# A gated mix of an S4 convolution and a two-token expert layer on one core: padded one-hot rows, spectra spread in place, a reloaded input, chunked expert weights, a split last block and new planner ranks

## The chip, the cores and the metric

The kernel runs on one core of a Trainium2 chip. The metric is the device time of one execution in microseconds (us), as the median of several runs. The profile is one further execution, taken by the hardware profiler; its times count from the first instruction.

## The reference, cut to what matters

The input `u` has 2048 time steps and 512 channels. Three results are mixed:

```
g = sigmoid((x * gate_w).sum(-1))                  # one gate per time step
a = conv(u, K) + u * Dskip                         # K[d,l] = Re sum_n C dB exp(dt A l)
r = x @ w_r;  idx = two largest of r               # the router picks 2 time steps
y = (silu(x[idx] @ w_gate) * (x[idx] @ w_up)) @ w_down * sigmoid(r[idx])
b = x + y scattered to the rows idx
out = g * a + (1 - g) * b
```

The convolution has 2048 taps per channel, each a sum over 128 complex states; the reference does it with an FFT of length 4096. The expert layer has a hidden width of 1792 and sees two rows only.

## The kernel before, in words

**Stages.** The channels are worked on in two halves of 256 (`h` = 0, 1), the time steps in two blocks of 1024 (`blk` = 0, 1).

1. ScalarE (ACT) and VectorE (DVE) build powers of the states: exponentials and sines (L638, L646, L721, L738) on ACT, their arguments (L643, L732) and the complex products (L617, L652, L668, L671) on DVE. ACT changes its function table between exponentials and sines.
2. TensorE (PE) transforms the input with a DFT matrix (L789, L792, tiles `x`), ACT evicts it (L796), and DVE forms sums and differences of the rows ("spread", L802), out of place from the tiles `eo` into the tiles `x`.
3. For each half PE multiplies the powers into taps (L838, L839; evicted L851), selects and regroups them (L863), and transforms them into the spectrum of the taps, `Kh` (L896; evicted L901), with the matrices `km`, loaded once for both halves (L811).
4. The router: PE transposes the input (L925), ACT evicts it (L928), PE forms the logits (L936). A chain of small steps on DVE, ACT and PE finds the two largest (L980 to L995), writes them as two one-hot columns into `oht` (L990, L996), transposes these to two rows `ohr` (L1013, L1016), gathers the two input rows by matmul against the input `u` (L1023), and runs the expert layer: L1050 for gate and up, L1056 to L1061 for the silu, L1066 for down, then three small steps that leave the result in row 0 and 1 of the tile `zb` (L1071 to L1073).
5. For each half and block, DVE multiplies the spectra ("Y", 16 or 8 operations over 128x2048 in bf16) and folds them; PE transforms back ("inv"): for each of 8 row groups one matmul adds the skip path (L1136), one adds the expert rows by the one-hot rows and `zb` (L1137), and eight are the transform (L1140). ACT scales (L1148) and SyncE (SP) stores.

**What sets the order.** Nothing is ordered by hand. Every operation is a node of a graph. A planner (L219) simulates the engines with a cost for each node, gives each engine the ready node of the highest rank (`RANKS`, L37) whose tiles fit into the SBUF, and so fixes the order of each engine's instructions and the waits between them (L324). On the chip each engine then runs its list strictly in order. The planner's SBUF budget is 4096 bytes a partition below the whole. `after=` adds a dependence: the loads of the expert weights, of the inverse DFT matrix and of the second copy of the input (L1078) come after the last tap matmul of the second half (`TAP1`); both sigmoids of the router wait for the last sine of the second half (`SINS`, L962, L1001). Every transform back waits for `zb`, since L1137 is in its accumulation group.

Of the kernel before, what the change touches and what calls it, by code (L numbers as in the profile page):

```python
# [24 lines left out]
MAGIC = 12582912.0  # L25
SB_BYTES = 212832


def bf16_bits(x):
# [55 lines left out]
class Op:  # L85
    __slots__ = ("name", "opts", "preds", "succs", "tiles", "prio", "npred", "ready", "eng", "start",
                 "fin", "idx", "mem", "dma", "bytes", "final", "num", "i", "pref", "clock")
# [35 lines left out]
def pack(tiles, size):  # L123

    near = {}
    for t in tiles:
        near[t.name] = [d for d in tiles if d is not t and d.t0 < t.t1 and t.t0 < d.t1]
    best = None
    for key in (lambda t: (-t.size * (t.t1 - t.t0), t.t0), lambda t: (-t.size, t.t0), lambda t: (-(t.t1 - t.t0), -t.size), lambda t: (t.t0, -t.size)):
        order = sorted(tiles, key=key)  # L130
        for _ in range(150):
            pos, top, worst = {}, 0, None
            for t in order:
                a = 0
                for lo, hi in sorted((pos[d.name], pos[d.name] + d.size) for d in near[t.name] if d.name in pos):
                    if a + t.size <= lo:
                        break
                    a = max(a, hi)
                pos[t.name] = a
                if a + t.size > top:  # L140
                    top, worst = a + t.size, t
            if best is None or top < best[0]:
                best = (top, pos)
            if top <= size:
                break
            k = order.index(worst)
            order.pop(k)
            order.insert(k // 2, worst)
        if best[0] <= size:
            break  # L150
    for t in tiles:
        t.addr = best[1][t.name]
    return best[0]


class Graph:
# [20 lines left out]
    def op(self, name, opts, reads=(), writes=(), pref=None, bias=0.0, after=(), hold=()):  # L177
        o = Op()
# [3 lines left out]
        o.i = len(self.ops)  # L182
        for a in after:
            o.preds[a.i] = a
# [34 lines left out]
    def schedule(self):  # L219
        ops = self.ops  # L220
# [21 lines left out]
        t = 0.0  # L242
        events = set()
        while left:
# [3 lines left out]
            while progress:  # L248
                progress = False
                for e in ENGS:  # L250
# [57 lines left out]
            if not nxt:  # L308
                if left:
                    w = sorted((o.name, [tl.name for tl in o.tiles if tl.t0 is None]) for e in ENGS for o in avail[e])  # L310
                    live = [(tl.name, tl.size) for tl in self.tiles if tl.t0 is not None and tl.t1 is None and tl.space == "sb"]
                    raise RuntimeError("no way on at %.1f: %s; live %s" % (t, w[:20], live))
                break
# [5 lines left out]
        if self.used > SB_BYTES:  # L319
            raise RuntimeError("needs %d bytes" % self.used)  # L320
        for tl in sb:
            tl.before = [o for d in sb if d.t1 <= tl.t0 and d.addr < tl.addr + tl.size and tl.addr < d.addr + d.size for o in d.ops]

# [155 lines left out]
def bass_gated_mix__ssm_conv_s4__moe_arch_mod__prompt_kernel(nc, A_u, A_A_re, A_A_im, A_B_re, A_B_im, A_C_re, A_C_im, A_log_dt, A_Dskip,  # L479
# [27 lines left out]
    with ExitStack() as es:  # L507
# [205 lines left out]
        for h in range(2):  # L713
# [27 lines left out]
            SINS = sins  # L741
            g.op("k0 im", {POOL: (lambda hh, ti=ti: hh.memset(ti(BF, 0, 128, 0, (128, NG), (1, 4)), 0.0), 0.5)}, [], [bk[0]], bias=100, after=sins[8:9])
# [27 lines left out]
        tEO = [[T("eo%d_%d" % (b, ri), 8192) for ri in range(2)] for b in range(2)]  # L770
        bEO = [[[Buf(tEO[b][ri]) for _ in range(4)] for ri in range(2)] for b in range(2)]
        tX = [[T("x%d_%d" % (b, ri), 8192) for ri in range(2)] for b in range(2)]
        bX = [[[Buf(tX[b][ri]) for _ in range(2)] for ri in range(2)] for b in range(2)]

        def eov(b, ri, row, *dims):
            return tEO[b][ri](BF, 0, 128, row * D, *dims)
        for b in range(2):
            for ri in range(2):
                for pr in range(4):
                    ps = PS("ps_x%d_%d_%d" % (b, ri, pr), 2)  # L780
                    bp = [Buf(ps) for _ in range(2)]
                    for i in range(2):
# [3 lines left out]
                        def mm(h, ps=ps, i=i, eo=eo, ri=ri, ft=ft, b=b, row=row):  # L786
# [8 lines left out]
                        XD.append(g.op("X%d row%d.%d" % (b, ri, row), {PE: (mm, 0.216 * (5 if b else 4))}, rd, [bp[i]], hold=[tEO[b][ri]]))  # L795
                    g.op("ev X%d.%d.%d" % (b, ri, pr), {ACT: (lambda h, ps=ps, b=b, pr=pr, ri=ri: h.activation(out=eov(b, ri, 2 * pr, (1, 1024)), in_=ps(F32, 0, 128, 0, (1, 1024)), func=ACTF.Copy), ca(1024, True)),  # L796
                                                        DVE: (lambda h, ps=ps, b=b, pr=pr, ri=ri: h.tensor_copy(eov(b, ri, 2 * pr, (1, 1024)), ps(F32, 0, 128, 0, (1, 1024))), cd(1024, x=2))},
                         bp, [bEO[b][ri][pr]], pref=ACT)
        for b in range(2):
            for ri in range(2):  # L800
                for sd in range(2):
# [408 lines left out]
```

## Time and profile before

| what | us |
|---|---|
| median of 3 runs (213.28 to 215.01) | 213.92 |
| the profiled execution's own time | 211.22 |
| its span, first to last instruction | 209.4 |
| DVE busy | 155.0 |
| PE busy | 145.9 |
| ACT busy | 136.0 |
| mean granted clock of PE | 0.868 of 2.4 GHz |

The profile page gives busy time by engine and in 40 slices; the queries of the trace give the chain of waits that ended last, the busy time of each engine in chosen stretches, and the instructions of an engine in order of time. A busy PE is not PE at its peak, since matmuls overlap; the distance from one start to the next is what a matmul costs.

### The profile page before, as it was taken

Reading aid. Unit: us, or ns where it says so; the run is one execution under the profiler, and the core shown is the slowest. Engines: PE = TensorE matmul, PEld = TensorE weight load, DVE = VectorE, ACT = ScalarE, POOL = GpSimd, SP = SyncE. Lnnn points to the kernel's source line nnn. Section 1 sums busy time; section 2 is a strip of 40 time slices with the busy share of each in tenths; the row PEclk is TensorE's granted clock in tenths of the full one; section 3 lists DMA queues with packets and bytes.
Section 4 is the critical chain, followed back from the end, with each engine's and each line's share of the span. In section 5 each row is a group of like instructions: output and inputs, shape, how many; then the busy total and the mean of one; then the engine's idle time right before and its main releaser. Section 6 shows DMA issues by size and latency. Waiting matters only on the chain.

```text
span 209.4 us, 3594 instructions
## 1 busy us (share of the span) xinstructions
PE 145.9 (70%) x1479; PEld 99.1 (47%) x1482; DVE 155.0 (74%) x249; ACT 136.0 (65%) x260; POOL 2.1 (1%) x10
## 2 busy tenths in 40 slices
PE   0508959972973894994011698997055999999993
PEld 0402424420453893872010697887012566666661
DVE  0497999949899999989798859999999993000000
ACT  2299999999699599799999595365003133333331
POOL 0000000000000000000000000000000000000000
PEclk9999999996797698899555599999558599999999
DMA  4994000000039300000000199992800011111111
GB/s 109 346 426 130 2 2 3 0 0 0 0 113 412 129 3 3 0 0 0 0 6 0 25 379 325 406 368 73 289 0 0 0 53 50 50 50 53 50 50 50
DMA packets 13923, 20.71 MB, mean 99 GB/s; under 512 B 4690, under 2 KB 10964, under 8 KB 12884
## 3 DMA queue, kind: packets, MB, share of 16 engines
q1 hardware_dynamic: 12564, 20.01, 26.8%
q10 hardware_dynamic: 1344, 0.49, 1.0%
q8 instruction: 11, 0.18, 0.3%
q14 instruction: 4, 0.03, 0.1%
HBM read 18.40 MB, written 2.10 MB: 98 GB/s over the span
## 4 chain that ended last, share of the span: by engine, by line
PE 42%; ACT 38%; DVE 13%; DMA 3%; issue 2%; ACTq 1%
PE RP L1140 16%; DVE RB L617 9%; ACT RB L721 8%; PE RP L896 7%; ACT RB L738 6%; ACT RB L796 5%; ACT RB L901 4%; PE RP L1137 3%; ACT RB L928 3%; DMA RB<-in_A_B_im_dram 3%; PE RP L838 3%; PE RP L839 2%; PE RP L1066 2%; ACT RB L638 2%; PE RP L1136 2%
## 5 line engine op out<-in xcount | busy, mean ns | idle before, releaser
L617 DVE TENSOR_TENSOR RB<-RB 128x2048 bf16<-128x2048 bf16 (+3 forms) x76 | 85.7, 1182 | 3.4 <-PE RP L839 1.8
L789 PE MATMUL RP<-RB 128*128 128x512 bf16 x125 | 34.4, 416 | 13.5 <-ACT RB L796 7.3
L1140 PE MATMUL RP<-RB 128*128 128x256 bf16 x256 | 35.8, 286 | 0.0
L1148 ACT ACTIVATE RB<-RP,RB 128x256 bf16<-128x256 f32 x32 | 13.4, 471 | 32.2 <-PE RP L1140 32.2
L789 PEld LDWEIGHTS RP<-RB 128*128 128x128 bf16 x128 | 12.9, 105 | 32.4 <-ACT RB L796 9.0
L896 PE MATMUL RP<-RB 128*128 128x256 bf16 x208 | 24.9, 283 | 4.4 <-ACT RB L874 3.6
L1140 PEld LDWEIGHTS RP<-RB 128*128 128x128 bf16 x256 | 23.4, 102 | 7.2 <-issue 0.7
L668 DVE TENSOR_TENSOR RB<-RB 128x1024 bf16<-128x1024 bf16 x40 | 25.2, 682 | 0.1
L896 PEld LDWEIGHTS RP<-RB 128*128 128x128 bf16 x208 | 20.7, 101 | 8.7 <-ACT RB L874 4.2
L721 ACT ACTIVATE RB<-RB 128x256 bf16<-128x256 f32 x62 | 20.3, 413 | 0.0
L901 ACT ACTIVATE RB<-RP 128x1024 bf16<-128x1024 f32 x16 | 15.8, 1030 | 6.5 <-PE RP L896 6.5
L738 ACT ACTIVATE RB<-RB 128x512 bf16<-128x512 int16 x32 | 17.6, 616 | 0.3 <-DVE RB L732 0.3
L796 ACT ACTIVATE RB<-RP 128x1024 bf16<-128x1024 f32 x16 | 15.5, 1012 | 1.6 <-PE RP L792 1.6
L838 PE MATMUL RP<-RB 128*128 128x84 bf16 x128 | 13.3, 224 | 4.0 <-DVE RB L617 2.6
L732 DVE TENSOR_SCALAR RB<-RB 128x256 int32<-128x256 f32 x49 | 11.7, 286 | 5.1 <-ACT RB L738 5.0
L838 PEld LDWEIGHTS RP<-RB 128*128 128x128 bf16 x128 | 12.6, 114 | 4.7 <-DVE RB L617 2.9
L851 ACT ACTIVATE RB<-RP 128x1008 bf16<-128x1008 f32 (+1 forms) x12 | 10.5, 910 | 4.4 <-PE RP L839 4.4
L839 PE MATMUL RP<-RB 128*128 128x84 bf16 x128 | 13.3, 223 | 0.0
L671 DVE TENSOR_TENSOR RB<-RB 128x1024 bf16<-128x1024 bf16 x20 | 12.9, 682 | 0.0
L839 PEld LDWEIGHTS RP<-RB 128*128 128x128 bf16 x128 | 12.6, 113 | 0.1
L1066 PE MATMUL RP<-RB 128*2 128x512 bf16 x14 | 4.9, 524 | 8.7 <-DVE RB L1061 8.7
L1136 PE MATMUL RP<-RB 128*128 128x256 bf16 x32 | 9.1, 286 | 2.2 <-ACT RB L955 2.2
(79 smaller groups left out, 147.0 us busy)
## 6 DMA issues: line engine op xcount, KB each, us to landing
RB<-in_A_u_dram SPq DMA_DIRECT2D x4, 1024.0 KB, 7.6
RB<-c_kspec SPq DMA_DIRECT2D x6, 512.0 KB, 6.4
RB<-c_fwd SPq DMA_DIRECT2D x2, 1024.0 KB, 9.6
RB<-c_inv SPq DMA_DIRECT2D x2, 1024.0 KB, 6.7
out_dram<-RB SPq DMA_DIRECT2D x8, 256.0 KB, 2.3
RB<-in_B_w_gate_dram SPq DMA_DIRECT2D x1, 1792.0 KB, 11.8
RB<-in_B_w_up_dram SPq DMA_DIRECT2D x1, 1792.0 KB, 15.7
RB<-in_B_w_down_dram SPq DMA_DIRECT2D x1, 1792.0 KB, 7.9
```

Source lines behind the costliest of these rows:

```text
L617: return g.op(name, {DVE: (lambda h: h.tensor_tensor(out=o(), in0=a(), in1=b(), op=op), cost)}, rd, wr, bias=bias, **kw)
L668: g.op("%s.m%d" % (name, i), {DVE: (lambda h, i=i, pa=pa, pb=pb: h.tensor_tensor(out=tv(i, inp_a[1]), in0=inp_a[0](pa), in1=inp_b(pb), op= ...
L721: e2.append(g.op("exp t1_%d %d" % (h, m), {ACT: (lambda hh, m=m, s=s, h=h: hh.activation(out=tT1[h](BF, 0, 128, s * 4, (128, NG), (1, 4)), ...
L738: sins.append(g.op("sin%d %d.%d" % (h, q, cs), {ACT: (lambda hh, ta=ta, cs=cs, tt_=tt_, q=q: hh.activation(out=tt_(BF, 0, 128, 8 * q, (4, ...
L789: r = h.matmul(o, tF(BF, 0, 128, ((j * 2 + ri) * 4 + ft) * 128, (1, 128)), tU(BF, 0, 128, (b * 8 + j) * D, (1, D)), start=(j == eo), stop= ...
L796: g.op("ev X%d.%d.%d" % (b, ri, pr), {ACT: (lambda h, ps=ps, b=b, pr=pr, ri=ri: h.activation(out=eov(b, ri, 2 * pr, (1, 1024)), in_=ps(F32 ...
L838: hh.matmul(o, tT1[h](BF, 0, 128, gr * 128, (1, 128)), t2v(h, 0, 0, (HC, NSL), (1, 4)) if gr == 0 else tT2[h](BF, 0, 128, 4 * gr, (HC, NSL ...
L839: r = hh.matmul(o, tTI[h](BF, 0, 128, gr * 128, (1, 128)), tT2[h](BF, 0, 128, NSL * HC + 4 * gr, (HC, NSL), (1, 4)), start=False, stop=True)
L896: r = hh.matmul(o, tKM[m](BF, 0, 128, c, (1, 128)), tKC[h](BF, 0, 128, u * 256, (1, 256)), start=(n == 0), stop=(n == len(steps) - 1))
L901: g.op("ev Kh %d.%d.%d" % (h, blk, pr), {ACT: (lambda hh, h=h, base=base, ps=ps: hh.activation(out=tKHH(h, base), in_=ps(F32, 0, 128, 0, ( ...
L1140: r = hh.matmul(o, tG(BF, 0, 128, ((j * 2 + ri) * 4 + ft) * 128, (1, 128)), tS(BF, 0, 128, (j % 2) * 2048 + ri * 1024 + ft * HC, (1, HC)), ...
L1148: r = hh.activation(out=tO(BF, 0, 128, i * 256, (1, 256)), in_=ps(F32, 0, 128, i * 256, (1, 256)), func=ACTF.Copy, scale=g32(0, 128, blk * ...
```

## The change

What it does, by parts: the one-hot columns stand 128 apart and the rows of `ohr` and `zb` are filled with zeros to 128 rows; the spread is written into one tile of nine 4096-byte slots that holds both the evicted transforms and the spread ones; the gather reads the second copy of the input, which is loaded after the first one-hot is there; the matrices `km` are loaded once for each half; the gate and up weights come in two chunks of columns each and the down weights in two chunks in tiles of their own, all after the last one-hot eviction (`GATE`); the router's sigmoids wait for the sines of the first half only (`SIN0`), the silu still for all; the last block (h = 1, blk = 1) is multiplied, folded and transformed back in two parts by frequency; the diagonal is made by 16 small operations. The planner gets new ranks, a larger SBUF margin (14336 bytes, raised until the tiles fit), another packing search, a cost for table loads and one for a cold PE. All ranks change; the diff shows a few.

```diff
-    ("tr u", 496), ("ev xt", 496), ("logits", 496), ... ("tr oh", 600), ("ev oh", 500), ("gather", 470), ... ("ffn", 470), ("h", 600), ... ("down", 600)
+    ("tr u", 926.9), ("ev xt", 810.0), ("logits", 810.0), ... ("tr oh", 356.6), ("ev oh", 348.1), ("gather", 925.3), ... ("ffn", 768.4), ("h", 803.1), ... ("down", 778.1)
-    ("Y0.0", 420), ("Y0.1", 410), ("inv 0", 400), ("ld w", 390), ("Y1.0", 320), ("Y1.1", 310), ("inv 1", 300)
+    ("Y0.0", 229.1), ("Y0.1", 509.1), ("inv 0", 303.0), ("ld w", 850.0), ("Y1.0", 848.4), ("Y1.1", 224.9), ("inv 1", 938.4)
...
+        for cut in range(CUT, 40000, 2048):
+            self.cap = SB_BYTES - cut
...
+                    if e == PE:
+                        if t - free[PE] > 3.0:
+                            warm = t + 5.0
+                        if t < warm:
+                            c = min(2 * c, c + (warm - t) / 2)
+                    if o.table and o.table != table:
+                        table = o.table
+                        c += 1.28
...
-        tEO = [[T("eo%d_%d" % (b, ri), 8192) for ri in range(2)] for b in range(2)]
-        tX = [[T("x%d_%d" % (b, ri), 8192) for ri in range(2)] for b in range(2)]
+        tXE = T("xe", 9 * 4096)
...
+                    over = (bEO[(i - 1) // 2][(i - 1) % 2][0:2] if i else []) if sd == 0 else bEO[b][ri][2:4]
+                    tt("spread %d.%d.%d" % (b, ri, sd), lambda xp=xp, sd=sd: tXE(BF, 0, 128, xp[sd] * 2048, (1, 2048)), ... bEO[b][ri], [bX[b][ri][sd]] + over, cd(2048))
...
-        tKM = [T("km%d" % u, 4096 if u < 6 else 2048, keep=430) for u in range(7)]
+        tKM = [[T("km%d_%d" % (u, h), 4096 if u < 6 else 2048, keep=(630, 490)[h]) for u in range(7)] for h in range(2)]
+            ld_km(h, xdone if h == 0 else T1DONE)
...
-        g.op("exp s", ..., [bSB], [bEx], after=SINS)
+        g.op("exp s", ..., [bSB], [bEx], after=SIN0)
...
-        dv("diag", lambda h: h.tensor_tensor(out=tDG(BF, 0, 128, 0, (128, 16), (1, 128)), ...
+            for tb in range(16):
+                r = h.tensor_scalar(out=tDG(BF, 0, 128, tb * 128, (1, 128)), in0=ident(), scalar1=rat(0, 128, tb, (1, 1)), scalar2=None, op0=ALU.mult)
...
-        tOH = T("oht", 64); bOH = Buf(tOH)
+        tOH = T("oht", 4096); bOH = Buf(tOH)
+        g.op("zero oh", {POOL: (lambda h: h.memset(tOH(BF, 0, 128, 0, (1, 2048)), 0.0), 2.5)}, [], [bOH], after=[LG0])
...
-                    r = h.transpose(ps(BF, 0, 2, i * 128, (1, 128)), tOH(BF, 0, 128, (hf * 8 + i) * 2, (1, 2)), ident())
+                    r = h.transpose(ps(BF, 0, 128, i * 128, (1, 128)), tOH(BF, 0, 128, (hf * 8 + i) * 128, (1, 128)), ident())
...
+        GATE = g.ops[-1:]
+            g.dma("ld U2_%d" % b, ..., 1048e3, writes=[bU2[b]], after=OH1)
-        g.op("gather", {PE: (gat, 4.8)}, bU + [bOH, bRatb], [bGt], bias=60)
+        g.op("gather", {PE: (gat, 2.3)}, bU2 + [bOH, bRatb], [bGt], bias=60)
-        tWG = T("wg", 14336); tWU = T("wu", 14336); tWD = tWG
+                tw = T("w%s%d" % ("gu"[i], c), 7168); bw = Buf(tw)
+                g.dma("ld w%s%d" % ("gu"[i], c), ..., 918e3, writes=[bw], after=GATE, bias=-10 * (2 * c + i))
+        tWD = [T("wd%d" % c, 7168) for c in range(2)]; bWD = [Buf(t) for t in tWD]
+            g.dma("ld wd%d" % c, ..., 918e3, writes=[bWD[c]], after=GATE, bias=-50 - 10 * c)
+        g.op("zero zb", {POOL: (lambda h: h.memset(tZB(BF, 0, 128, 1024, (1, D)), 0.0), 0.6)}, [], [bZB[2]], after=[LG0])
...
+                nparts = 2 if (h, blk) == (1, 1) else 1
+                nr = 4 // nparts
+                for pt in range(nparts):
...
-                                hh.matmul(o, tOR(BF, 0, 2, tb * 128, (1, 128)), tZB(BF, 0, 2, 1024 + h * HC, (1, HC)), start=False, stop=False)
+                                    if pt == 0:
+                                        hh.matmul(o, tDG(...), tU2[blk](...), start=(jj == 0), stop=False)
+                                        hh.matmul(o, tOR(BF, 0, 128, tb * 128, (1, 128)), tZB(BF, 0, 128, 1024 + h * HC, (1, HC)), start=False, stop=False)
+                                    for ft in range(pt * nr, pt * nr + nr):
```

## Rows read from the trace of the kernel before

**Rows 1.** The page, busy time by engine, and PE's granted clock in 40 slices.
```profile
PE 145.9 (70%) x1479; PEld 99.1 (47%) x1482; DVE 155.0 (74%) x249; ACT 136.0 (65%) x260; POOL 2.1 (1%) x10
...
PEclk9999999996797698899555599999558599999999
```

**Rows 2.** The chain of waits that ended last: start us, length us, what.
```profile
153.98 4.90 PE RP L1066 x14
...
161.06 0.40 PE RP L1136
...
205.81 0.47 ACT RB L1148
206.29 0.36 ACTq L507
```

**Rows 3.** Busy time by stretch: from:to, length, engines (instructions), PE clock, DMA share, GB/s.
```profile
0.00:113.80 113.80, 68.28 (x614) 42.55 (x617) 97.54 (x183) 99.60 (x187) 2.08 (x10) 0.86 0.22 77
113.80:174.40 60.60, 46.22 (x625) 35.29 (x626) 57.45 (x67) 25.46 (x48) 0.00 (x0) 0.81 0.45 166
...
161.00:205.80 44.80, 44.72 (x320) 29.59 (x320) 13.40 (x12) 12.59 (x31) 0.00 (x0) 0.93 0.14 42
...
130.00:140.00 10.00, 9.26 (x88) 8.16 (x85) 10.00 (x10) 4.95 (x8) 0.00 (x0) 1.00 1.01 408
```

**Rows 4.** DVE in order of time: start us, length us, instruction, count, idle before.
```profile
7.82 0.69 DVE L600 SCALAR_TENSOR_TENSOR RB<-RP,RB 128x512 f32<-128x512 bf16 x1 [7.82 <-PE RP L584]
...
92.77 2.49 DVE L668 TENSOR_TENSOR RB<-RB 128x1024 bf16<-128x1024 bf16 x4
...
142.12 2.28 DVE L972 TENSOR_TENSOR RB<-RB 128x2048 bf16<-128x2048 bf16 x1
144.33 5.76 DVE L617 TENSOR_TENSOR RB<-RB 128x2048 bf16<-128x2048 bf16 x5
...
153.79 20.65 DVE L617 TENSOR_TENSOR RB<-RB 128x2048 bf16<-128x2048 bf16 x18
```

**Rows 5.** PE and its weight loads in order of time, one row group of the transform back.
```profile
187.83 1.05 PE L1140 MATMUL RP<-RB 128*128 128x256 bf16 x8
188.71 0.27 PE L1136 MATMUL RP<-RB 128*128 128x256 bf16 x1
188.92 0.28 PE L1137 MATMUL RP<-RB 2*128 2x256 bf16 x1
189.13 1.05 PE L1140 MATMUL RP<-RB 128*128 128x256 bf16 x8
...
188.91 0.09 PEld L1137 LDWEIGHTS RP<-RB 2*128 2x128 bf16 x1 [0.21 <-issue]
```

**Rows 6.** PE, ACT and POOL in order of time, around router, expert layer and spectrum.
```profile
51.10 1.89 PE L789 MATMUL RP<-RB 128*128 128x512 bf16 x4 [5.20 <-ACT RB L796]
...
105.96 1.01 PE L936 MATMUL RP<-RB 128*128 128x2 bf16 x32 [9.00 <-ACT RB L928]
...
122.41 1.05 PE L1013 MATMUL RP<-RB 128*2 128x128 bf16 x16
...
130.92 11.53 PE L896 MATMUL RP<-RB 128*128 128x256 bf16 x104 [0.74 <-ACT RB L874]
142.28 3.00 PE L1050 MATMUL RP<-RB 128*128 128x2 bf16 x112
...
66.72 1.97 ACT L928 ACTIVATE RB<-RP 128x1024 bf16<-128x1024 bf16 x2
...
112.90 0.63 ACT L738 ACTIVATE RB<-RB 128x512 bf16<-128x512 int16 x1 [0.33 <-DVE RB L732]
...
49.67 0.31 POOL L742 MEMSET RB<- 128x256 bf16 x1 [19.52 <-ACT RB L738]
```

**Rows 7.** DMA issues: tensors, queue, count, KB each, us from issue to landing.
```profile
RB<-in_A_u_dram SPq DMA_DIRECT2D x4, 1024.0 KB, 7.6
...
RB<-in_B_w_up_dram SPq DMA_DIRECT2D x1, 1792.0 KB, 15.7
```

More of the change, by code (lines that the diff above doesn't have):

```diff
@@ L86 @@
     __slots__ = ("name", "opts", "preds", "succs", "tiles", "prio", "npred", "ready", "eng", "start",
-                 "fin", "idx", "mem", "dma", "bytes", "final", "num", "i", "pref", "clock")
+                 "fin", "idx", "mem", "dma", "bytes", "final", "num", "i", "pref", "clock", "table")
 class Mem:
@@ L120, in take, with pack, place @@
         return before
[L123 to L152, printed above, removed]
+def pack(tiles, size, iters=1500, seed=0):
+    n=len(tiles); rnd=random.Random(seed)
+    near=[[j for j in range(n) if j!=i and tiles[j].t0<tiles[i].t1 and tiles[i].t0<tiles[j].t1] for i in range(n)]
+    sz=[t.size for t in tiles]
+    def place(order,limit):
+        pos=[None]*n; top=0; worst=-1
+        for i in order:
+            iv=sorted((pos[j],pos[j]+sz[j]) for j in near[i] if pos[j] is not None)
+            a=0
+            for lo,hi in iv:
+                if a+sz[i]<=lo: break
+                if hi>a: a=hi
+            pos[i]=a
+            if a+sz[i]>top: top=a+sz[i]; worst=i
+        return top,worst,pos
+    keys=(lambda t:(-t.size*(t.t1-t.t0),t.t0),lambda t:(-t.size,t.t0),lambda t:(-(t.t1-t.t0),-t.size),lambda t:(t.t0,-t.size))
+    best=None
+    for k in keys:
+        order=sorted(range(n),key=lambda i:k(tiles[i]))
+        r=place(order,size)
+        if best is None or r[0]<best[0]: best=(r[0],order,r[2],r[1])
+    cur=best
+    for it in range(iters):
+        if best[0]<=size: break
+        top,order,pos,worst=cur
+        o2=list(order)
+        if rnd.random()<0.7:
+            hi=[i for i in range(n) if pos[i]+sz[i]>size-(0 if rnd.random()<.5 else 20000)] or [worst]
+            w=rnd.choice(hi); k=o2.index(w); o2.pop(k); o2.insert(rnd.randrange(0,k+1),w)
+        else:
+            a,b=rnd.randrange(n),rnd.randrange(n); o2[a],o2[b]=o2[b],o2[a]
+        r=place(o2,size)
+        if r[0]<=cur[0] or rnd.random()<0.02:
+            cur=(r[0],o2,r[2],r[1])
+            if r[0]<best[0]: best=cur
+    for i in range(n):
+        tiles[i].addr = best[2][i]
@@ L182, in op @@
         o.i = len(self.ops)
+        o.table = next((w for w in ("exp", "sin") if name.startswith(w)), None)
         for a in after:
@@ L219, in schedule, with fill @@
     def schedule(self):
+        prios = [o.prio for o in self.ops]
+        for cut in range(CUT, 40000, 2048):
+            self.cap = SB_BYTES - cut
+            self.order = {e: [] for e in ENGS}
+            for o, p in zip(self.ops, prios):
+                o.prio = p
+            for tl in self.tiles:
+                tl.addr = tl.t0 = tl.t1 = tl.free_t = None
+                tl.before = []
+                tl.left = len(tl.ops)
+            if self.fill():
+                return
+        raise RuntimeError("needs %d bytes" % self.used)
+    def fill(self):
         ops = self.ops
@@ L319, in schedule @@
         if self.used > SB_BYTES:
-            raise RuntimeError("needs %d bytes" % self.used)
+            return False
         for tl in sb:
             tl.before = [o for d in sb if d.t1 <= tl.t0 and d.addr < tl.addr + tl.size and tl.addr < d.addr + d.size for o in d.ops]
+        return True
     def link(self, sems, newsem):
@@ L961, in bass_gated_mix__ssm_conv_s4__moe_arch_mod__prompt_kernel @@
         bOm, om_ = rs(16, BF); bRat, rat = rs(16, F32); bRatb, ratb = rs(16, BF); bO32, o32 = rs(16, F32); bRcg, rcg = rs(16, F32)
-        g.op("exp s", {ACT: (lambda h: h.activation(out=ex_(), in_=sb_(), func=ACTF.Exp, scale=-1.0), ca(16))}, [bSB], [bEx], after=SINS)
+        g.op("exp s", {ACT: (lambda h: h.activation(out=ex_(), in_=sb_(), func=ACTF.Exp, scale=-1.0), ca(16))}, [bSB], [bEx], after=SIN0)
         dcp("den", de_, ex_, [bEx], [bDe], bias=1.0)
@@ L1000, in bass_gated_mix__ssm_conv_s4__moe_arch_mod__prompt_kernel @@
         bMe = Buf(tLG); bMd = Buf(tLG); bMg = Buf(tLG)
-        g.op("exp ms", {ACT: (lambda h: h.activation(out=ms(0, 128, 1, (1, 1)), in_=ms(0, 128, 0, (1, 1)), func=ACTF.Exp, scale=-1.0), ca(1))}, [bMs], [bMe], after=SINS, bias=60)
+        g.op("exp ms", {ACT: (lambda h: h.activation(out=ms(0, 128, 1, (1, 1)), in_=ms(0, 128, 0, (1, 1)), func=ACTF.Exp, scale=-1.0), ca(1))}, [bMs], [bMe], after=SIN0, bias=60)
         dcp("ms den", lambda: ms(0, 128, 2, (1, 1)), lambda: ms(0, 128, 1, (1, 1)), [bMe], [bMd], bias=1.0)
@@ L1056, in bass_gated_mix__ssm_conv_s4__moe_arch_mod__prompt_kernel @@
+        tWD = [T("wd%d" % c, 7168) for c in range(2)]; bWD = [Buf(t) for t in tWD]
+        for c in range(2):
+            g.dma("ld wd%d" % c, lambda h, c=c: h.dma_start(tWD[c](BF, 0, 128, 0, (D, 7), (1, D)), dr(B_w_down, c * 7 * 128 * D, (D, 128), (128 * D, 7), (1, D))), 918e3, writes=[bWD[c]], after=GATE, bias=-50 - 10 * c)
+        dcp("hg", hg, lambda: psH[0](F32, 0, 128, 0, (1, 28)), bH[0], [bHg])
+        dcp("hu", hu, lambda: psH[1](F32, 0, 128, 0, (1, 28)), bH[1], [bHu])
         g.op("exp h", {ACT: (lambda h: h.activation(out=he(), in_=hg(), func=ACTF.Exp, scale=-1.0), ca(28))}, [bHg], [bHe], after=SINS)
```

209 lines of the change are left out of this document (114 added, 95 removed), and 27 rows, old and new, of the table RANKS.

## The prediction

> **What bounds the kernel now.** I read the chain of waits first, from its end. From 161.06 us to 205.81 us it is PE alone, in the transform back; before that comes the expert layer's down product at 153.98 us [rows 2]. So the end is set by two things in a row: when the expert result `zb` is there, and how long 320 matmuls of the transform take after it.
>
> Then the busy time by stretch. Up to 113.80 us ACT is busy 99.60 and DVE 97.54; from there to 174.40 us DVE is busy 57.45 of 60.60, PE only 46.22; from 161.00 to 205.80 us PE is busy throughout, and ACT and DVE are not [rows 3]. In order of time DVE starts at 7.82 us and its last operation ends at 153.79 + 20.65 = 174.44 us [rows 4]. Of these 166.6 us it is busy 155.0 [rows 1], idle 11.6. The reader is to see a DVE that is nearly full until 174.4, and 35 us after it in which PE catches up with work whose spectra had been ready for long: the transform is late because it waits for `zb`, not for DVE.
>
> **The end before.** The last scale starts at 205.81 us and the span ends at 209.4: 3.6 us for scale, store and closing. The execution's own time is 211.22, 1.82 above its span; the median of the runs is 213.92, 2.70 more. So a span is turned into a median by + 4.5.
>
> **Padding to 128 rows.** Within a row group, L1136 starts at 188.71, L1137 at 188.92, the next L1140 at 189.13, and eight L1140 take 188.71 - 187.83 = 0.88 [rows 5]. A matmul of 128 rows thus costs 0.11, and going into and out of the one with 2 rows costs 0.21 each, with 0.21 of "issue" idle ahead of its weight load. With 128 rows both steps should be 0.11: 0.20 less of 1.30 for a row group, 32 groups, 6.4 us of PE. The bounds are 0 and 6.4, with no loss, since the neighbours of full height show what such a matmul costs; I take 6.4, because those 8 a group are the nearest rows. The transform back is then 32 x 1.10 = 35.2 us at the full clock. Before it took 44.8 [rows 3] against 32 x 1.30 = 41.6, so 3.2 us were the cold start (the granted clock is 0.5 in the slice from 162 to 167 us, [rows 1]).
> On this one rule speaks against the change. The Trainium skill, "TensorE: Matmul & The Clock Gate", section "LDWEIGHTS (loading the stationary operand)", says that the contraction rows don't matter to a weight load, only its columns. The duration of the load agrees (0.09 us with 2 rows, [rows 5]), but the idle 0.21 ahead of it isn't covered by that rule; by the rule alone the padding would save nothing.
> The memset of 2048 columns for the one-hots runs on POOL: 8 times the 0.31 of 256 columns [rows 6] is at most 2.5 us, beside the search for the largest that follows the logits; cost nothing, and 2.5 us on the way to `zb` if that search is shorter. The transposes have the same 16 instructions and their evictions the same columns.
>
> **The router and expert layer, earlier.** This is the large part. Six of eight evictions of the transposed input were done by 66.72 + 1.97 = 68.7 us, but the logits ended only at 105.96 + 1.01 = 107.0 us, for want of the last two [rows 6]. In the new ranks these evictions stand above nearly all of ACT's work, so the logits can end near 68.7 + 2 x 0.98 + 1.0 = 72 us. From there to the transposes of the one-hots it took 122.41 - 107.0 = 15.4 us [rows 6]; so one-hots can be there at 87. Their transposes and evictions, however, now have nearly the lowest ranks, and ACT is full until its last sine, which ends at 112.90 + 0.63 = 113.5 us [rows 6]. So `GATE` opens between 88 and 114; I take 114, the late end, because ACT is busy 99.60 of the 113.80 us before [rows 3].
> Behind `GATE` come 6 loads, 5.5 MB together. The DMA moved 408 GB/s when full [rows 3]: 13.5 us, plus some 2 us for the first, so about 129. (The second load before, 1.8 MB among 7.7, took 15.7 us [rows 7]: the same size.) The input's second copy, 7.6 us a load [rows 7], lies ahead of that, behind the first one-hot. The same 2 MB were loaded before, so it adds no bytes. The second load of `km` adds 3.4 MB, 8 us of a DMA that is idle around 100 us.
> From 142.28 (gate and up) to 161.06 took 18.8 us [rows 2, 6], of which DVE put 5.76 [rows 4] of "Y" work ahead of one little step of the silu. In the new ranks the silu stands above "Y0.0", "Y0.1" and "Y1.1", so a step waits for one operation of 1.15 at most; I take 18.8 - 5.8 = 13. So `zb` is there at 129 + 13 = 142 us. Bounds: 126.5 (last sine + 13) and 153 (114 + 15.5 + the whole 18.8, and 5 us for the 2.1 MB of the inverse DFT, at 408 GB/s, if they stand ahead). The queue that is passed is SP's, which issues nearly every load and store in one list: a load that waits for `GATE` holds those planned behind it, the inverse DFT among them.
>
> **DVE.** The last block's 16 operations of 1.15 become 32 of half size at 2.49 / 4 = 0.62 [rows 4]: + 1.4. The diagonal was 2.28 [rows 4]; 16 small ones lie between 16 x 0.09 (what is left of 0.62 and 1.15 when the columns go to none: 2 x 0.62 - 1.15) and 16 x 0.2: - 0.8 to + 0.9; I take 0. Spreading in place issues the same 8 operations; its extra dependences fall on evictions long done. So DVE needs 155.0 + 1.4, starts at 7.8, and with the idle time of before ends at 175.8. What this idle will be under a new order is the greatest unknown: not under 3 (the first waits are for sines), and 8 more than before if the loads `F0` and `F1`, now issued behind both blocks of the input, delay ACT's first evictions, or the smaller SBUF budget holds work back. I keep 11.6, the row's value, since ACT sets the pace of the first 113 us in either order.
>
> **PE against it.** With `zb` at 142, `Kh` of the second half (11.53 us, [rows 6]) is just done, as before at 142.4. Three blocks and the first part of the last are 35.2 - 32 x 0.11 = 31.7 us, with a cold start of 3.2: 176.9. DVE's last fold ends at 175.8, a little before: PE has not been idle, and the second part runs at the full clock: 32 matmuls, 3.5 us, to 180.4. (Had PE waited some 5 us for DVE, it would run at half the clock, as after the 5.20 idle at 51.10 [rows 6], and need 7.0.)
> Sum: 180.4 + 3.6 = 184.0 of span; + 4.5 = **188.5** as a median, against 213.92.
>
> **Rivals.**
> *The expert result stays late.* The chain has as many handoffs as before and a gate that lies behind ACT; if `zb` still comes at 161, PE is the bound: 161.06 + 3.2 + 35.2 + 3.6 = 203.1, median 207.6. For it: the low rank of the one-hot evictions. Against it: 35 us of slack between 72 and 107 in the logits. Chance 0.09, and 0.03 that it comes a little later still and the time is within 1% (211.8 to 216.1, about what a measurement can tell from no change).
> *Padding gives nothing*: the 2-row weight load stalls for another reason than its height. Then PE needs 41.6 + 3.2 after 142: 186.8 + 3.6 = 190.4, median 195. This is how it would go by the Trainium skill's section named above. Against it: the steps of 0.21. Chance 0.06.
> *DVE loses its idle time.* With only 3 us idle and `zb` by 132: 7.8 + 156.4 + 3 = 167.2, and 3.5 + 3.6 after it: 174.3, median 179. Chance 0.10.
> *Slower: the weights wait for room.* The six chunks no longer share a buffer (43,008 bytes a partition instead of 28,672, in a smaller budget). If they find room only when Kh of the second half ends at 142.45 [rows 6], they land at 142.45 + 15.5 = 158, `zb` comes at 171 to 177, and the end is 177 + 3.2 + 35.2 + 3.6 = 219, median 223.5. It decides against the change from a `zb` at 170. Against it: the transforms and spread rows give up 28,672 bytes (36,864 for 65,536). Chance 0.05.
> *The reorder falls short in between*, `zb` near 150 or DVE 8 us idler: 150 + 3.2 + 35.2 + 3.6 = 192, median 196.5. Chance 0.22. The forecast itself, 183 to 193: 0.45.
>
> **Numbers.** The range goes from 178 to 199: the low end is the case of little idle time, the high end a `zb` at 153 (195.0 + 4.5 = 199.5). Left out are the late expert result, no change and slower, 0.17 together, and little below. Faster by over 1%: 0.92; within 1%: 0.03; slower: 0.05.
>
> **What would show it.** In the profile after: L1136, the one-hot matmul and the transform's matmuls all 0.11 apart at the full clock; logits ending before 80 us; the first inverse matmul before 150 us, with DVE still multiplying; DVE ending within a few us of 175; only one part of one block, some 32 matmuls, after DVE's last fold. I am wrong if the first inverse matmul is still near 161, or if DVE shows over 20 us of idle time after its start.

## The result, and the profile after

The changed kernel takes 178.36 us (median; 177.89 to 183.21), the kernel before 213.6 beside it (211.51 to 215.01): a ratio of 0.8376, 95% interval [0.8306, 0.8446]. The forecast was 188.5 with a range of 178 to 199. The execution profiled first was a disturbed one (span 181.4), so the rows of after come from a later execution of the same kernel, span 176.8 and time 178.64.

The page, busy time by engine and PE's granted clock in 40 slices, against [rows 1]:
```profile
PE 132.4 (75%) x1479; PEld 101.1 (57%) x1482; DVE 158.2 (89%) x287; ACT 133.0 (75%) x253; POOL 4.3 (2%) x12
...
PEclk9999999999999965999996555599999999999998
```
PE is busy 13.5 us less, DVE 3.2 more, and DVE is now at 89% of the span instead of 74. The slices of half clock lie at 97 to 115 us and around 66 to 71, before the transform back; in it the clock is full.

The chain of waits that ended last, from its last long pieces on (start us, length us, what), against [rows 2]:
```profile
138.65 29.52 DVE RB L660 x40
169.54 3.68 PE RP L1213 x32
...
173.25 0.47 ACT RB L1224
```
Where 45 us of PE alone stood, there are now 30 us of DVE, then 32 matmuls of the last part on PE, and the same 3.6 us (176.8 - 173.25) behind the last scale's start.

Busy time by stretch (from:to, length, PE, PEld, DVE, ACT, POOL with instructions, PE clock, DMA share, GB/s), against [rows 3]:
```profile
0.00:113.80 113.80, 74.05 (x788) 50.88 (x792) 104.42 (x209) 104.05 (x198) 4.29 (x12) 0.88 0.38 138
...
137.20:173.20 36.00, 35.44 (x322) 31.06 (x319) 32.25 (x44) 14.72 (x33) 0.00 (x0) 1.00 0.15 45
```
In the first 113.8 us DVE does 104.42 instead of 97.54 and ACT 104.05 instead of 99.60: what DVE had to do behind 113.8 shrank there already. In the transform back both PE (35.44 of 36.00) and DVE (32.25) are nearly full.

PE in order of time (start us, length us, instruction, count, idle before), against [rows 5, 6]:
```profile
64.46 1.01 PE L989 MATMUL RP<-RB 128*128 128x2 bf16 x32 [2.70 <-ACT RB L981]
...
116.05 0.84 PE L1113 MATMUL RP<-RB 128*128 128x2 bf16 x28
...
130.58 3.18 PE L1131 MATMUL RP<-RB 128*2 128x512 bf16 x14
133.69 3.67 PE L949 MATMUL RP<-RB 128*128 128x256 bf16 x32
137.20 0.27 PE L1209 MATMUL RP<-RB 128*128 128x256 bf16 x1
137.31 0.27 PE L1210 MATMUL RP<-RB 128*128 128x256 bf16 x1
137.42 1.04 PE L1213 MATMUL RP<-RB 128*128 128x256 bf16 x8
138.29 0.27 PE L1209 MATMUL RP<-RB 128*128 128x256 bf16 x1
...
142.20 0.28 PE L1209 MATMUL RP<-RB 128*128 128x256 bf16 x1 [0.47 <-DVE RB L660]
```
The logits end at 65.5 instead of 107.0, the first gate product starts at 116.05, the down product ends at 133.8, and the first inverse matmul starts at 137.20 instead of 161.06, straight behind the last of `Kh`. A row group takes 138.29 - 137.20 = 1.09 instead of 1.30. One wait for DVE of 0.47 us is left.

The last of the three small steps that leave the expert result in `zb`, in ACT's order of time:
```profile
135.95 0.70 ACT L1008 ACTIVATE RB<-RB 2x512 bf16<-2x512 bf16 x1
```
So `zb` is there at 136.65, before PE has ended `Kh`: the transform back no longer waits for it.

DVE at its end, against [rows 4]:
```profile
7.16 0.69 DVE L645 TENSOR_TENSOR RB<-RP,RB 128x512 f32<-128x512 bf16 x1 [7.16 <-PE RP L627]
...
129.24 2.69 DVE L1027 TENSOR_SCALAR RB<-RB 128x128 bf16<-128x128 bf16 x16
131.84 37.64 DVE L660 TENSOR_TENSOR RB<-RB 128x2048 bf16<-128x2048 bf16 x48
```
DVE starts at 7.16 and ends at 131.84 + 37.64 = 169.48. Of these 162.3 us it is busy 158.2, so idle 4.1; before it was 11.6.

SyncE's queue from 100 to 125 us, what it waited for (us in total, times, longest us):
```profile
SPq L1107 <- PE RP L892: 6.7, 1, 6.7
```
The gate weights were issued at 108.55, but the up and down weights behind them only from 116.25 on, after 6.7 us in which the queue waited for the last taps of the second half.

### The profile page after: what moved, and what is told of

Same layout as the page of the kernel before. It is cut to its first block, busy times and chain, and to the rows that moved or that the text cites. A ratio compares the mean times of both kernels' runs of the same rounds, so it can differ in the third digit from the quotient of the medians.

```text
span 181.4 us, 3637 instructions
## 1 busy us (share of the span) xinstructions
PE 136.8 (75%) x1479; PEld 103.0 (57%) x1482; DVE 158.1 (87%) x287; ACT 133.0 (73%) x253; POOL 4.3 (2%) x12
## 4 chain that ended last, share of the span: by engine, by line
PE 42%; ACT 38%; DVE 8%; DMA 7%; issue 3%; SPq 0%; ACTq 0%; DVEq 0%
PE RP L1213 15%; ACT RB L764 9%; PE RP L949 8%; ACT RB L841 7%; DVE RB L660 5%; ACT RB L689 5%; ACT RB L954 4%; DMA RB<-in_B_w_gate_dram 4%; ACT RB L782 4%; PE RP L916 3%; DMA RB<-in_A_A_im_dram 3%; ACT RB L681 2%; PE RP L891 2%; PE RP L892 2%; ACT RB L981 2%
## 5 line engine op out<-in xcount | busy, mean ns | idle before, releaser
L660 DVE TENSOR_TENSOR RB<-RB 128x2048 bf16<-128x2048 bf16 (+4 forms) x92 | 86.5, 1002 | 1.1 <-ACT RB L841 1.0
L834 PE MATMUL RP<-RB 128*128 128x512 bf16 x126 | 33.6, 408 | 12.9 <-DVE RB L660 10.2
L1213 PE MATMUL RP<-RB 128*128 128x256 bf16 x256 | 33.3, 273 | 0.0
L834 PEld LDWEIGHTS RP<-RB 128*128 128x128 bf16 x128 | 12.9, 103 | 30.6 <-DMA RB<-c_fwd 10.5
L1224 ACT ACTIVATE RB<-RP,RB 128x256 bf16<-128x256 f32 x32 | 13.4, 470 | 20.5 <-PE RP L1213 20.4
L949 PE MATMUL RP<-RB 128*128 128x256 bf16 x208 | 26.6, 291 | 1.7 <-ACT RB L954 0.8
L1213 PEld LDWEIGHTS RP<-RB 128*128 128x128 bf16 x256 | 25.0, 98 | 3.1 <-DVE RB L660 0.2
L949 PEld LDWEIGHTS RP<-RB 128*128 128x128 bf16 x208 | 20.9, 104 | 6.5 <-ACT RB L954 1.1
L764 ACT ACTIVATE RB<-RB 128x256 bf16<-128x256 f32 x62 | 20.7, 413 | 0.0
L954 ACT ACTIVATE RB<-RP 128x1024 bf16<-128x1024 f32 x16 | 15.2, 1013 | 6.5 <-PE RP L949 6.5
L782 ACT ACTIVATE RB<-RB 128x512 bf16<-128x512 int16 x32 | 17.7, 619 | 0.1
L891 PE MATMUL RP<-RB 128*128 128x84 bf16 x128 | 13.7, 233 | 4.0 <-DVE RB L660 4.0
L891 PEld LDWEIGHTS RP<-RB 128*128 128x128 bf16 x128 | 13.5, 119 | 4.1 <-DVE RB L660 4.1
L841 ACT ACTIVATE RB<-RP 128x1024 bf16<-128x1024 f32 x15 | 15.2, 1024 | 0.0
L892 PE MATMUL RP<-RB 128*128 128x84 bf16 x128 | 13.7, 232 | 0.0
L892 PEld LDWEIGHTS RP<-RB 128*128 128x128 bf16 x128 | 13.5, 119 | 0.0
L904 ACT ACTIVATE RB<-RP 128x1008 bf16<-128x1008 f32 (+1 forms) x11 | 10.0, 958 | 2.5 <-PE RP L892 2.4
L689 ACT ACTIVATE RB<-RB 128x512 bf16<-128x512 int16 x16 | 8.7, 619 | 0.0
L1209 PE MATMUL RP<-RB 128*128 128x256 bf16 x32 | 8.7, 273 | 0.0
```

The costliest lines, as they stand in the source:

```text
L660: return g.op(name, {DVE: (lambda h: h.tensor_tensor(out=o(), in0=a(), in1=b(), op=op), cost)}, rd, wr, bias=bias, **kw)
L689: s1.append(g.op("sin z%d.%d" % (t, hh_), {ACT: (lambda h, ta=ta, i=i, hh_=hh_: h.activation(out=tZ[hh_](BF, 0, 128, i * 512, (256, 2), (1 ...
L782: sins.append(g.op("sin%d %d.%d" % (h, q, cs), {ACT: (lambda hh, ta=ta, cs=cs, tt_=tt_, q=q: hh.activation(out=tt_(BF, 0, 128, 8 * q, (4, ...
L834: r = h.matmul(o, tF(BF, 0, 128, ((j * 2 + ri) * 4 + ft) * 128, (1, 128)), tU(BF, 0, 128, (b * 8 + j) * D, (1, D)), start=(j == eo), stop= ...
L891: hh.matmul(o, tT1[h](BF, 0, 128, gr * 128, (1, 128)), t2v(h, 0, 0, (HC, NSL), (1, 4)) if gr == 0 else tT2[h](BF, 0, 128, 4 * gr, (HC, NSL ...
L892: r = hh.matmul(o, tTI[h](BF, 0, 128, gr * 128, (1, 128)), tT2[h](BF, 0, 128, NSL * HC + 4 * gr, (HC, NSL), (1, 4)), start=False, stop=True)
```

## The experiments

Times are medians; a ratio is to the kernel before on the same chip. The terms of the forecast are tested first by undoing one part (e1 to e3), then by putting one part into the kernel before (e4 to e7), then with the order of the work held fixed (e9, e10), and last by trying to be faster (e12). Spans are those of the one profiled execution of a run, so a difference of spans is given beside that of the medians.

**e0_after**, the changed kernel again, as the base of e1 to e3.

> The changed kernel as it is, for a second profile beside the runs below. The profile on record has a span of 181.4 us and a time of 183.2, its other runs 177.9 to 178.8. Theory (expert result and padding): first matmul of the transform back near 142 us, PE without a gap from there, 320 matmuls in 35.2 us. Where the 5 us between its runs lie is not known: if it is the expert weights' transfer, the first gate matmul moves from 117.2 to about 112; if it is the clock, PE's stretches have another granted clock.

Measured 179.82, span 176.8, ratio 0.8594 [0.848, 0.8709]. Its rows are those above. The first inverse matmul came at 137.20 where 142 was expected, and the transform back took 36.0 us. The first gate product came at 116.05, not near 112, and the clock of the transform back is 1.00 in both profiles, so where the 5 us between executions lie stays open.

**e1_two_rows**, the change with the 2-row matmul in the transform back.
```
- tOR(BF, 0, 128, tb * 128, (1, 128)), tZB(BF, 0, 128, 1024 + h * HC, (1, HC))
+ tOR(BF, 0, 2, tb * 128, (1, 128)), tZB(BF, 0, 2, 1024 + h * HC, (1, HC))
```

> The one-hot matmul of the transform back uses 2 rows again; everything else, the order of every engine included, is that of the changed kernel. Theory (the step into and out of a 2-row matmul costs 0.10 us each, 32 times, and PE has no slack after 142 us): 6.4 us longer than the changed kernel run beside it, and 0.21 us from start to start around that matmul. Rival (rows don't matter to a weight load): within 0.5 us. Second rival (DVE sets the end, PE's backlog is hidden): 0 to 3 us longer.

Measured 184.64, span 182.8, ratio 0.8822 [0.8764, 0.888]: 6.0 more of span than e0_after, 4.8 more by the medians. PE in order of time, one row group:
```profile
137.38 0.27 PE L1209 MATMUL RP<-RB 128*128 128x256 bf16 x1
137.59 0.28 PE L1210 MATMUL RP<-RB 2*128 2x256 bf16 x1
137.80 1.05 PE L1213 MATMUL RP<-RB 128*128 128x256 bf16 x8
138.68 0.27 PE L1209 MATMUL RP<-RB 128*128 128x256 bf16 x1
```
The steps are 0.21 and 0.21 again, the group 1.30, with everything up to 137.4 as it was. Both rivals are refuted: the rows make a difference, and DVE's work does not hide it. Of 32 x 0.21 = 6.7 us, 0.7 of span were hidden: in the padded kernel PE waits a little for DVE, here never. The stationary and the moving operand lose their rows together here, so which of them makes the step dearer was not separated.

**e2_one_part**, the last block in one part.
```
- nparts = 2 if (h, blk) == (1, 1) else 1
+ nparts = 1
```

> The last block is multiplied, folded and transformed back in one part again, ranks and all else as in the changed kernel. Theory (the end is DVE's last fold plus what PE has left): DVE ends 1.4 us earlier, but 80 matmuls (8.8 us) instead of 32 (3.5 us) come after it: 3.9 us longer, and up to 7 if PE has waited and runs at half the clock. Rival (PE's backlog from 142 us sets the end, the parts only change the order): within 1 us.

Measured 186.38, span 184.9, ratio 0.8904 [0.8836, 0.8971]: 8.1 more of span than e0_after, 6.6 more by the medians, where 3.9 to 7 was expected. PE in order of time at the end:
```profile
169.43 0.40 PE L1209 MATMUL RP<-RB 128*128 128x256 bf16 x1 [4.24 <-DVE RB L660]
...
171.53 0.42 PE L1209 MATMUL RP<-RB 128*128 128x256 bf16 x1
```
and the busy time of two stretches of it (columns as above):
```profile
169.40:175.60 6.20, 6.17 (x30) 4.45 (x31) 0.00 (x0) 0.84 (x2) 0.00 (x0) 0.51 0.00 0
175.60:181.30 5.70, 5.66 (x52) 4.82 (x50) 0.00 (x0) 1.68 (x4) 0.00 (x0) 1.00 0.15 46
```
DVE ends at 169.4, not 1.4 us earlier as expected, and behind it stand 80 matmuls instead of 32, and PE has been idle for 4.24 us: the granted clock is 0.51 (the level of 1.2 GHz) for 6.2 us, a group takes 2.10 there, and then it is 1.00. So of the 8.1 us some 5.3 are 48 more matmuls at 0.11, and 3 the clock. The second part is worth more than its half-block, because the first part keeps PE going while DVE works.

**e3_old_ranks**, the change with the list of ranks of before.

> The changed kernel with the ranks of the kernel before; dependences, tiles, padding, parts and the planner's costs are those of the change. Theory (most of the gain is the earlier expert result, and that comes from the order): the result comes at 150 to 162 us, the time is 192 to 206. Rival (the dependences that were taken away bring it, the sigmoids' wait and the chunked loads): result before 147 us, time within 5 us of the changed kernel.

Measured 200.47, span 197.2, ratio 0.9607 [0.947, 0.9743]. Two pieces of its chain of waits:
```profile
137.94 13.72 DMA RB<-in_B_w_down_dram
151.71 4.58 PE RP L1126 x14
```
The weights are issued at 134 to 136, the down product starts at 151.71, the first inverse matmul at 158.45, and PE is full for 35.2 us after it. That is the late expert result of the forecast's rival, with its price: 20.4 us of span more than e0_after, 20.7 by the medians.

What DVE waited for in this kernel (us in total, times, longest us):
```profile
DVE RB L638 <- PE RP L622: 8.0, 1, 8.0
DVE RB L655 <- ACT RB L949: 2.1, 2, 1.6
```
and three lines behind the first of the same view of the next kernel, e4_new_ranks_only:
```profile
DVE RB L857 <- PE RP L844: 5.3, 1, 5.3
DVE RB L622 <- ACT RB L906: 4.7, 1, 4.7
DVE RB L737 <- ACT RB L743: 4.4, 3, 2.3
```
The reader is to see that DVE's idle time behind its first wait is short in e3 with the old ranks (2.8 us in all) and long in e4 with the new ones (19.1). So the ranks are neither needed nor enough to take the idle time away; the rest of the change is: tiles, dependences, small operations or the planner's new costs. These were not taken apart. How busy ACT is does not decide it either: in the first 113.8 us ACT is busy 93.47 in e3 and 104.44 in e4, less and more than the 99.60 of before.

**e4_new_ranks_only**, the kernel before with the list of ranks of the change.

> The kernel before with the ranks of the change and nothing else. Theory (order and dependences need each other: the expert weights and the sigmoids still wait for the last taps and sines, so the result can't come before 150 us): 198 to 212 us. Rival (the order alone brings the gain): below 190 us.

Measured 201.31, span 200.1, ratio 0.9617 [0.9529, 0.9705]. PE in order of time:
```profile
134.59 4.50 PE L1071 MATMUL RP<-RB 128*2 128x512 bf16 x12 [1.21 <-DVE RB L1066]
...
143.20 11.53 PE L901 MATMUL RP<-RB 128*128 128x256 bf16 x104 [0.74 <-ACT RB L879]
154.57 0.27 PE L1141 MATMUL RP<-RB 128*128 128x256 bf16 x1
```
The time came out as expected, the reason did not: the expert result was there at 140, but the taps and `Kh` of the second half came behind it, and the transform back started at 154.6 with groups of 1.30. By the ratios, each to the kernel before on its own chip, the ranks alone gain 3.8%, the rest without the ranks (e3) 3.9%, both together 14.1% (e0_after): each alone leaves another thing late ahead of the transform back.

**e5_before_padded**, the kernel before with all one-hot operations of 128 rows and the two memsets; the planner is free to reorder.

> The kernel before with one-hot rows and expert rows filled to 128 rows, nothing else changed on purpose; the planner's order shifts a little. Theory: 6.4 us shorter than before, since the end there is PE alone. Rival (rows don't matter to a weight load): no difference beyond 1 us.

Measured 221.96, span 218.0, ratio 1.0602 [1.0437, 1.0768]. PE in order of time:
```profile
170.51 4.96 PE L1067 MATMUL RP<-RB 128*2 128x512 bf16 x14 [7.42 <-DVE RB L1062]
```
A miss, and no test of padding: the planner, given other tiles, put the down product at 170.51 instead of 153.98, which cost more than the padding gives.

**e6_before_no_expert**, the kernel before, the transform back taking a tile of zeros in place of `zb`, so that it doesn't wait for the expert layer; planner free.
```
- tZB(BF, 0, 2, 1024 + h * HC, (1, HC))
+ tZZ(BF, 0, 2, h * HC, (1, HC))
```

> The kernel before, whose transform back reads a tile of zeros in place of the expert rows: the expert layer still runs, but nothing waits for it and its result is left out of the output. Theory (before, the end was set by the late expert result, and without it DVE sets the end): first inverse matmul before 140 us, DVE's last operation near 174, then one block of 80 matmuls at 0.13, 10.4 us, up to 3.2 of cold start, and 3.6: span 188 to 192, time 190 to 196. Rival (PE's total work or another wait holds the transform back): above 203 us.

Measured 205.64, span 201.3, ratio 0.973 [0.9623, 0.9838]. PE in order of time:
```profile
136.76 13.18 PE L896 MATMUL RP<-RB 128*128 128x256 bf16 x104 [2.65 <-issue]
...
152.65 0.27 PE L1138 MATMUL RP<-RB 128*128 128x256 bf16 x1
```
The expected 188 to 192 of span failed, and the rival came out: the new plan moved `Kh` from 130.92 to 136.76, and the transform back, which stands behind `Kh` and the gate and up products on PE, to 152.65. Without the wait for `zb`, `Kh` is the next to hold it.

**e7_after_no_expert**, the same edit on the changed kernel; planner free.

> The changed kernel, whose transform back reads a tile of zeros in place of the expert rows: the expert layer still runs, its result is left out of the output. Theory (in the changed kernel DVE sets the end, 158 us busy from 7.5 us on and 3.7 + 3.6 us behind its last fold): within 3 us of the changed kernel (179 us). Rival (the expert result still sets the end): 5 us or more shorter.

Measured 190.66, span 188.4, ratio 0.9117 [0.9033, 0.9201], slower than with the expert layer in the way, which neither theory nor rival expected. In its new order PE's first inverse matmul waits for the matrix of the inverse DFT:
```profile
144.12 0.39 PE L1211 MATMUL RP<-RB 128*128 128x256 bf16 x1 [2.06 <-DMA RB<-c_inv]
```
Two kernels that were meant to get lighter, e5 and e7, came out 6% slower than the kernel that they start from (e5 1.0602 of before; e7 0.9117 of before, where the changed kernel, on another chip, had 0.8594). An edit of a few lines lets the planner lay out the whole kernel anew, and that is larger than what was to be measured. So in e9, e10 and e12 each engine's list of operations was fixed to that of the kernel that the edit starts from. e9 and e10 also take the packing search of the change in place of that of before.

**e9_before_pinned_padded**, e5 with the order of before on every engine.

> The kernel before with 128 one-hot and expert rows, and with every engine's instruction order held to that of the kernel before (e5 let the planner reorder, and the expert result came later). Theory (0.20 us less for each of 32 row groups, the end being PE alone): 6.4 us less than before, 1.09 us from group to group instead of 1.30. Rival (rows don't matter to a weight load): no difference beyond 1 us.

Measured 210.05 (206.05 to 211.94), beside 211.99 for before; the rows are of an execution of 209.46, span 207.7. PE in order of time:
```profile
112.36 1.02 PE L950 MATMUL RP<-RB 128*128 128x2 bf16 x32 [9.01 <-ACT RB L942]
...
167.23 0.28 PE L1152 MATMUL RP<-RB 128*128 128x256 bf16 x1 [2.19 <-ACT RB L969]
...
173.27 0.27 PE L1152 MATMUL RP<-RB 128*128 128x256 bf16 x1
...
174.36 0.27 PE L1152 MATMUL RP<-RB 128*128 128x256 bf16 x1
```
The median barely moved, but two things cancel in the profiled execution. From the first inverse matmul to the last scale it takes 204.04 - 167.23 = 36.8 us instead of 44.75 [rows 2], 7.9 less. Of these, 6.1 are the padding in the 29 groups at the full clock, 1.09 instead of 1.30; the other 1.9 lie in the first three groups, in part because the clock in the first 6 us was 0.72 here and 0.50 in before. And all the work is some 6 us late, the logits at 112.36 instead of 105.96. This starts in the first 25 us, where no one-hot is in play. DVE in order of time:
```profile
13.34 0.69 DVE L631 TENSOR_TENSOR RB<-RP,RB 128x512 f32<-128x512 bf16 x1 [2.83 <-ACT RB L626]
```
The small input `B_im` landed 8.9 us after its issue instead of 6.2, and the first transform then waited for one of ACT's sines until 22.10 (before, it started at 16.27). In e5 and e6 it waited for a sine as well, until 19.8, with `B_im` landing after 6.5, so the late landing is not all of it. The tiles lay at other addresses in this kernel and the next; whether that is the cause was not run. The execution of 206.05 has no profile, so whether it starts late too is not known; it is 5.9 below the median of before.

**e10_before_pinned_no_wait**, e6 with the order of before, the down product moved behind the transform back.

> The kernel before in its own order, but the transform back reads zeros in place of the expert rows, and the down product with its three steps stands behind it on PE and ACT; the expert result is left out of the output. Theory (before, the late expert result cost what lies between the end of gate and up and 161 us): first inverse matmul at 145 to 147 us, then 41.6 us of PE without a gap, span 190 to 193, time 192 to 196, so some 16 to 19 us of the gain belong to the expert result. Rival (DVE or the spectrum of the second half holds the transform back as well): above 200.

Measured 200.96 (197.09 to 202.09), beside 211.99 for before; the rows are of an execution of 200.66, span 198.9. PE in order of time:
```profile
137.02 11.53 PE L910 MATMUL RP<-RB 128*128 128x256 bf16 x104 [0.74 <-ACT RB L888]
...
151.25 0.27 PE L1152 MATMUL RP<-RB 128*128 128x256 bf16 x1
```
In time it missed the expectation: the median lies above the 200 of the rival, the shortest execution 1.1 us above the theory's 196. In the profile it is the same late start, `Kh` at 137.02 instead of 130.92, and `Kh` is what holds the transform back then. Behind `Kh` it is as the theory has it: the transform back starts 151.25 - 137.02 = 14.2 us after `Kh`, where in before it was 161.06 - 130.92 = 30.1, and PE is full from there. So the wait for `zb` held the transform back by 15.9 us in the kernel before, with PE's groups as they were.

**e0b_after**, the changed kernel once more, as the base of the last run.

> The changed kernel again, as the base of the next run on the same chip: 178 to 180 us.

Measured 179.26, span 177.5, ratio 0.8481 [0.8438, 0.8524].

**e12_diag_act_warm**, the change with its order fixed, the diagonal on ACT, and 12 matmuls of 384 columns, whose result nobody reads, ahead of the second half's taps.
```
- dv("diag", dgf, [bRat, bSM], [bDG], cost=16 * 0.105)
+ for tb in range(16): h.activation(out=tDG(...), in_=ident(), func=ACTF.Copy, scale=rat(0, 128, tb, (1, 1)))
+ for _ in range(12): h.matmul(psW(F32, 0, 128, 0, (1, 384)), ident(), tSM(...), start=True, stop=True)
```

> The changed kernel in its own order with two edits: the 16 small operations of the diagonal run on ACT behind the last tap eviction instead of on DVE, and 12 matmuls of 384 columns without use stand between the gather and the taps of the second half, where PE is idle. Theory (in the changed kernel DVE and PE set the end together, DVE by its 158 us of work and PE by the chain from the taps on, whose first 6 us run at half the clock): DVE's last fold 2 to 3 us earlier, the taps at the full clock within 3 us of their start, the time 2 to 3 us shorter. Rival (one of the two alone sets the end, through a wait that neither edit touches): within 0.8 us.

Measured 179.47, span 177.4, ratio 0.8493 [0.8446, 0.854]: no gain over e0b_after, where 2 to 3 us were expected. Busy time by stretch (columns as above) of e0b_after, ahead of the gate product:
```profile
109.00:116.00 7.00, 6.84 (x110) 6.85 (x111) 6.97 (x8) 4.63 (x8) 0.00 (x0) 0.57 0.76 259
```
and of e12, the same stretch and the one behind the gate product:
```profile
109.00:116.00 7.00, 6.44 (x184) 6.35 (x188) 6.67 (x8) 6.88 (x14) 0.00 (x0) 1.00 0.84 275
121.30:125.00 3.70, 3.67 (x44) 2.90 (x45) 3.11 (x5) 0.73 (x4) 0.00 (x0) 0.55 1.09 381
```
The extra matmuls did their part: 0.57 became 1.00, and the first gate product came at 113.92 instead of 116.70. ACT in order of time, and PE and DVE behind it, show what ate it:
```profile
115.05 4.78 ACT L1037 ACTIVATE RB<-RB 128x128 bf16<-128x128 bf16 x16
119.74 1.00 ACT L927 ACTIVATE RB<-RP 128x1024 bf16<-128x1024 f32 x1
...
121.33 2.02 PE L955 MATMUL RP<-RB 128*128 128x256 bf16 x10 [2.19 <-ACT RB L933]
...
131.46 1.23 DVE L666 TENSOR_TENSOR RB<-RB 128x2048 bf16<-128x2048 bf16 x1 [1.46 <-ACT RB L960]
133.20 36.51 DVE L666 TENSOR_TENSOR RB<-RB 128x2048 bf16<-128x2048 bf16 x47 [0.52 <-ACT RB L960]
```
The diagonal takes ACT 4.78 us in one piece; the eviction that `Kh` needs waits behind it, PE waits 2.19 and falls back to 0.55 of the clock, and DVE, 2.3 us lighter, waits 1.46 + 0.52 us, and 0.76 more earlier, for ACT. It ends at 169.71 instead of 170.12. In this kernel relieving DVE by loading ACT gave nothing. The two edits were not run apart, so what the extra matmuls alone would give is open. No kernel here was faster than the changed one.

## Why the forecast was right, and where it was off

The direction, the mechanism and the order of the steps were right; the time was 10.1 us too high. Step by step:

- **What bounds the kernel before**: shown. Without the wait for `zb` the transform back starts 15.9 us earlier behind `Kh` (e10), and with the expert result late again the changed kernel loses 20.4 (e3).
- **Padding**, 6.4 us: by undoing it 6.0 of span and 4.8 by the medians (e1), and 0.21 for each row group at the full clock in the kernel before (e9). The steps of 0.21 became 0.11 as taken from the neighbours of full height. The Trainium skill's rule ("TensorE: Matmul & The Clock Gate", section "LDWEIGHTS (loading the stationary operand)") is that the rows of a weight load don't matter to its time. The trace agrees for the load's own duration, 0.09 us with 2 rows [rows 5] and 0.10 with 128 (e0_after); the 0.21 of idle ahead of the load with 2 rows lies outside that rule, and the rival that drew "no gain" from it is refuted by e1.
- **The transform back**, 35.2 us: 36.0 from 137.20 to 173.20. The **cold start** of 3.2 was not paid: the clock was 1.00 in all of it, with `Kh` running straight into it. The forecast had the cold start in its sum although its own `Kh` ended at 142.4, right where it let the transform begin.
- **`zb` at 142**: 136.65, and the first inverse matmul at 137.20. Logits at 65.5 (forecast 72); the weights issued from 108.55 on (`GATE` was put at 114). From `GATE` to `zb` 28 was forecast and 136.65 - 108.55 = 28.1 is what it took, but that the two agree is luck, since the terms were others. There were 6.7 us in which the up and down weights waited behind the taps, which the forecast did not name for this place; by the graph they need only `GATE`, so it is of the kind of its rival "the weights wait for room", 6.7 us long instead of 28. And the silu's last product was done at 127.0, but PE's list had 44 matmuls of `Kh` ahead of the down product, which started at 130.58.
- **DVE ends at 175.8**: 169.48. This is the single term that was off most. The idle time of before, 11.6, was carried over "since ACT sets the pace of the first 113 us in either order"; 4.1 was left. The 5.0 us that DVE had waited for one line of ACT, in four places of before, are nearly gone. The reason given does not hold: in e3 ACT is less busy than before in these 113.8 us and DVE has 2.8 us of idle time, in e4 ACT is busier and DVE has 19.1. The busy time was 158.2 where 156.4 was forecast, 1.8 more; 0.4 of it are the diagonal's 16 small operations, 2.69 against 2.28. So - 7.5 + 1.8, and - 0.6 for the earlier start, make the 6.3 between 175.8 and 169.5.
- **The second part**, 3.5 us behind DVE: 3.68. The **end** of 3.6: 3.6. The forecast's sum went by PE, at 176.9 ahead of the last part. In fact PE was there at 169.3, earlier by the 4.8 of the transform's start and the 3.2 of the clock, less short waits, and DVE at 169.48: the two met. Had only one of them come early, the other would have kept the span near 183 or 184.
- **From span to median**, + 4.5: 1.8 (178.64 - 176.8). The 2.7 by which the median of before stood above its profiled execution did not carry over. 184.0 became 176.8, which is 7.2; 2.7 for this; together 9.9 of the 10.1.

The rival "DVE loses its idle time" (179) gave the time, with a chance of 0.10: its wording wanted 3 us of idle and `zb` by 132, and got 4.1 and 136.65. The band of the forecast itself, 183 to 193, was missed, and 178.36 lies 0.4 above the lower end of the range. The forecast kept a stall of the old order although it knew that every rank was new. What took the idle time away is open beyond what e3 and e4 show. Of the parts of the change, the padding, the split block and the ranks were undone one by one; the spread in place, the second copy of the input, the second load of `km`, the chunked weights, the earlier sigmoids and the planner's costs were not, so what each of them gives is not known.

## What to carry to other kernels

Follow the last chain of the profile to the one input that starts it, and ask what each engine would end at without it; here PE, freed of `zb`, ended within 4 us of DVE, and splitting the last block was what made the two overlap. Don't carry an engine's idle time from one order to another: price the busy time, and let the idle time be a range. Where a planner lays out the program, hold every engine's order fixed before a single edit is timed: with it free, two kernels meant to get lighter came out 6% slower. Even then look where the stretches begin to differ, since a late start of 6 us hid what the padding gave in the profile of e9.

## What was not expected of the hardware

- Sixteen multiplications of 128x128 by a column took 2.69 us on DVE (0.17 each) and 4.78 on ACT (0.30 each, e12).
- 12 matmuls of 384 columns, 3.56 us long, ahead of the taps brought the granted clock from 0.57 to 1.00 in the 7 us behind them; a wait of 2.19 us some 10 us later was followed by 0.55 (e12), while one of 2.19 us ahead of the transform back of e3 was followed by 1.00.
- The load of `B_im`, 128 KB, landed 8.9 and 8.8 us after its issue in the profiles of e9 and e10, and 5.4 to 6.5 in the twelve others. Why was not run.
